# Batches 0 and 1 of q and k loaded as 2 KB runs and regrouped on chip; band mask by matmul, two AV buffers, idle matmuls ahead of the data, new filler counts, two output tiles

## The chip, the cores and the metric

The kernel runs on one core of a Trainium2 chip. The metric is device time in microseconds (us) of one launch. Each version was executed several times; the kernel before takes 373.0 to 375.9 us. The profile is one of those executions, and its span is about 2 us shorter than the time. Engines: PE is TensorE (matmul), PEld its weight loads, DVE VectorE, ACT ScalarE, POOL GpSimd, SP the queue that stores the output.

## The reference, cut to what matters

```
q, k, v: [8 batches, 8 heads, 576 tokens, 64] f32
out_d    = softmax attention over means of 4 tokens (144 per head), repeated 4 times
out_local= softmax attention over tokens with |i - j| < 4 (a band)
x   = (out_d + out_local) as [4608, 512]
out = gelu(x @ w_in) @ w_out          # w_in 512x2048, w_out 2048x512
```

The kernel works in 9 chunks of 512 tokens. `m1(c)` is the first matmul of chunk c with its Gelu, `m2(c)` the second, 64 matmuls of 128x512 each, 0.216 us apiece at full clock. While chunk c is in m1, batch c+1 is brought in (transposed, summed in fours); while it is in m2, batch c+1 goes through attention. Batch 0 has nothing to hide behind: it is the prologue.

## The kernel before

The parts that matter: batch 0's loads are 256-byte runs, the band mask is built by six selections on GpSimd (POOL) and multiplied in by VectorE, and large matmuls ("fillers") are placed between the steps of the attention so that TensorE doesn't wait.

```python
def load_qk0(p):                                   # batch 0: 16 DMAs of 256-byte runs
    for nm, src in (("qn", q), ("kn", k)):
        for h in (2 * p, 2 * p + 1):
            nc.gpsimd.dma_start(out=ld[0][nm][:, :, h, :],
                                in_=src[0, h].rearrange("(c s) d -> s c d", s=CH))
# ... cut ...
def t_in(b, p, which):                             # batches 1 to 7: tokens to columns
    tr = ppool.tile([128, 1024], F16, tag="tr")    # one buffer
    for c in range(NCK):                           # 6 transposes of 96 tokens
        nc.tensor.transpose(tr[:, CH*c:CH*c+CH], nat[:, c, 2*p:2*p+2, :], I128[0:CH, 0:CH])
    # ... q: copy to qT, sums of four; k: two copies to kz, sums of four to kdz (cut)
# ... cut ...
def attn(b, fill, n0, n1, n2):
    fill(n0); scores(b, 0); fill(n1); mask(0); s_lo(b)
    for p in range(NP):
        if p + 1 < NP:
            scores(b, p + 1)
            if p + 2 == NP: to_gelu()              # ScalarE's table, 1.28 us
        else:
            fill(2)
        av(b, p)
        if p + 1 < NP: mask(p + 1)
        fill(n2)                                   # 7
        t_out(b, p)                                # transposes nall, the result of av
# ... cut ...
osb = wpool.tile([128, 512], F32, tag="osb", bufs=3)   # output tiles
```

The softmax here doesn't subtract the row's maximum and nothing guards it: scores larger than these inputs give would overflow.

## Time and profile before

| stage, from the timeline | us |
|---|---|
| prologue (batch 0), up to the first m1 matmul | 39.8 |
| chunk 0, input part of batch 1 beside m1 | 22.0 |
| chunk 0, attention of batch 1 beside m2 | 26.0 |
| six steady periods (batches 2 to 7) | 225.7 (37.6 each) |
| last two chunks and the end | 59.2 |
| span | 372.7 |

The windows view gives the two parts of chunk 0. Columns: window, length, busy time of PE, PEld, DVE, ACT and POOL with instruction counts, granted TensorE clock (1.00 is full), mean busy DMA share, GB/s.

```profile
39.80:61.80 22.00, 19.47 (x114) 8.58 (x113) 13.49 (x24) 9.23 (x16) 13.54 (x18) 0.88 1.76 162
61.80:87.80 26.00, 22.60 (x224) 13.08 (x223) 14.37 (x22) 13.09 (x26) 16.01 (x18) 1.00 1.18 110
```

TensorE's clock can be read from the length of equal matmuls. These lines are of the timeline of the kernel before (start, length, engine, line, operation, tiles, shapes, count, and in brackets the idle time and what ended it):

```profile
12.62 0.49 PE L298 MATMUL sc<-qT,kz 128*128 128x116 f16 x3
...
24.50 0.59 PE L252 MATMUL vd_ps<-v_win,Gb 128*128 128x512 f16 x1 [0.23 <-DMA v_win<-in_v_dram]
...
39.76 8.44 PE L170 MATMUL m_ps<-xT,w_in_sb 128*128 128x512 f16 x26
```

The same three score matmuls take 0.32 us in a group later on. So the prologue ran at half clock up to about 28 us, although the windows view writes 1.00 for it; m1 also began at half clock: 26 matmuls in 8.44 us, where full clock needs 5.6. The second line shows what batch 0 waited for: v_win, which landed at 24.5 us.

In the steady periods TensorE had one clear wait. The chain of waits of one period (start, length, what) leaves TensorE after the last scores, goes through ScalarE and VectorE, and comes back with the last output transpose:

```profile
148.29 0.19 PE tr_o L351
...
152.43 0.23 PE sc L304 x4
...
153.04 0.73 ACT e L312
...
154.25 1.00 ACT L365
...
155.75 0.47 ACT out_sb L193
156.22 0.19 ACT xd L357
...
156.43 0.76 DVE xT L358
157.19 0.16 DVE rr L342
...
157.38 1.10 DVE nall L344
...
158.53 0.23 PE tr_o L351
```

From the end of the last scores (152.66) to the last transpose (158.53) are 5.9 us, and the filler work placed there is about 1 us too short.

### The profile page before, as it was taken

How to read it: one execution, taken by the hardware profiler on the slowest of the kernel's cores; microseconds unless marked ns; L12 is line 12 of the kernel's file. 1: busy time of each engine (PE TensorE's matmuls, PEld its weight loads, DVE VectorE, ACT ScalarE, POOL GpSimd, SP SyncE). 2: the span in 40 equal slices, each digit the busy share in tenths (PEclk: the TensorE clock that was granted, in tenths of full speed). 3: DMA queues.
4: the chain of work that ended last, by engine and by line, in shares of the span. 5: the costliest groups of instructions: out<-in, count | busy, mean ns of one | idle time of the engine just before them, and what ended most of it. 6: DMA issues, size and time to landing. Idle time of an engine off the chain costs nothing.

```text
span 372.7 us, 6854 instructions
## 1 busy us (share of the span) xinstructions
PE 337.7 (91%) x2812; PEld 187.1 (50%) x2812; DVE 186.1 (50%) x318; ACT 193.3 (52%) x366; POOL 187.8 (50%) x254
## 2 busy tenths in 40 slices
PE   1764888879999999999999999999999999999995
PEld 1634344545565556555554556455645564444442
DVE  5327278483757276728672857285728572000000
ACT  2634244554575457545763676357635763623721
POOL 8993937761396639662976298529762100000000
PEclk9998599999999999999999999999999999999999
DMA  7999999991099809980999099909990002002002
GB/s 50 83 147 190 138 194 134 140 95 58 0 97 155 124 2 93 162 123 2 88 163 126 2 80 165 131 1 78 166 132 2 4 30 84 0 30 84 0 30 84
DMA packets 134383, 32.30 MB, mean 87 GB/s; under 512 B 118608, under 2 KB 129872, under 8 KB 134352
## 3 DMA queue, kind: packets, MB, share of 16 engines
q0 software_dynamic: 129024, 22.43, 78.3%
q1 hardware_dynamic: 5184, 9.31, 7.0%
q8 instruction: 22, 0.36, 0.4%
q10 hardware_dynamic: 144, 0.13, 0.1%
q14 instruction: 9, 0.07, 0.1%
HBM read 44.83 MB, written 9.44 MB: 146 GB/s over the span
## 4 chain that ended last, share of the span: by engine, by line
PE 75%; DVE 9%; ACT 7%; POOL 5%; issue 2%; DMA 1%; ACTq 0%; DVEq 0%; POOLq 0%
PE m_ps L170 32%; PE m_ps L182 27%; DVE nall L344 3%; PE sc L298 3%; ACT L365 2%; DVE xT L358 2%; PE sc L304 2%; PE tr_o L354 2%; PE tr_k L202 2%; PE tr_q L202 2%; ACT e L312 2%; POOL k_nat L106 2%; POOL q_nat L106 2%; PE tr_o L351 1%; DMA v_win<-in_v_dram 1%
## 5 line engine op out<-in xcount | busy, mean ns | idle before, releaser
L170 PE MATMUL m_ps<-xT,w_in_sb 128*128 128x512 f16 x576 | 137.7, 384 | 0.0
L182 PE MATMUL m_ps<-w_out_sb,gT 128*128 128x512 f16 x576 | 133.9, 379 | 0.0
L173 ACT ACTIVATE gT<-m_ps 128x512 f16<-128x512 f32 x144 | 86.0, 597 | 59.3 <-PE m_ps L170 59.3
L182 PEld LDWEIGHTS <-gT 128*128 128x128 f16 x576 | 53.5, 98 | 57.3 <-issue 1.0
L170 PEld LDWEIGHTS <-w_in_sb 128*128 128x128 f16 x576 | 53.7, 99 | 56.8 <-issue 3.6
L212 POOL TENSOR_TENSOR q_t<-qT 128x288 f32<-128x288 f16 x24 | 16.0, 665 | 66.2 <-DVE qT L205 51.9
L193 ACT COPY out_sb<-m_ps 128x512 f32<-128x512 f32 x35 | 20.5, 586 | 44.6 <-PE m_ps L182 44.6
L221 DVE TENSOR_REDUCE kdz<-kz 64x144 f16<-64x576 f16 x56 | 41.8, 747 | 1.8
L83 POOL DMA_DIRECT2D q_nat<-in_q_dram x42 | 32.6, 790 | 10.1 <-PE m_ps L170 4.2
L344 DVE TENSOR_TENSOR nall<-av,rr 128x896 f16<-128x896 f32 x32 | 34.9, 1091 | 1.1
L358 DVE TENSOR_TENSOR xT<-tr_o,xd 128x576 f16<-128x576 f16 x32 | 24.2, 758 | 21.5 <-ACT xd L357 21.5
L217 DVE COPY kz<-tr_k 64x576 f16<-64x576 f16 x56 | 25.4, 454 | 18.4 <-PE tr_k L202 17.5
L83 POOL DMA_DIRECT2D k_nat<-in_k_dram x42 | 32.2, 783 | 4.6 <-DMA w_in_sb<-in_moe_w_in_dram 3.6
L320 DVE TENSOR_TENSOR e<-e,band 128x1152 f16<-128x1152 f16 x32 | 24.7, 773 | 16.6 <-ACT e L313 16.0
L205 DVE COPY qT<-tr_q 128x576 f16<-128x576 f16 x28 | 12.8, 458 | 36.4 <-PE tr_q L202 35.7
L188 DVE COPY out_sb<-m_ps 128x256 f32<-128x256 f32 x1 | 0.4, 425 | 58.4 <-PE m_ps L182 58.4
L357 ACT COPY xd<-tr_o 128x144 f16<-128x144 f16 x32 | 8.9, 279 | 38.1 <-PE tr_o L354 38.1
L95 POOL DMA_DIRECT2D v_win<-in_v_dram x30 | 26.7, 927 | 1.3 <-DMA k_nat<-in_k_dram 1.3
L312 ACT ACTIVATE e<-sc 128x680 f16<-128x680 f32 x32 | 23.4, 732 | 0.0
L351 PE MATMUL tr_o<-I,nall 128*128 128x128 f16 x32 | 7.5, 233 | 14.5 <-DVE nall L344 13.9
L272 POOL TENSOR_TENSOR v_t<-v_grp 128x1024 f32<-128x1024 f16 x6 | 12.7, 2115 | 14.5 <-DMA v_grp<-in_v_dram 14.5
L313 ACT ACTIVATE e<-sc 128x472 f16<-128x472 f32 x32 | 18.2, 570 | 0.0
(91 smaller groups left out, 397.8 us busy)
## 6 DMA issues: line engine op xcount, KB each, us to landing
out_dram<-out_sb SPq DMA_DIRECT2D x35, 256.0 KB, 3.4
v_win<-in_v_dram POOLq DMA_DIRECT2D x40, 128.0 KB, 9.5
q_nat<-in_q_dram POOLq DMA_DIRECT2D x42, 96.0 KB, 4.0
k_nat<-in_k_dram POOLq DMA_DIRECT2D x42, 96.0 KB, 4.6
v_grp<-in_v_dram POOLq DMA_DIRECT2D x6, 512.0 KB, 8.4
w_in_sb<-in_moe_w_in_dram POOLq DMA_DIRECT2D x4, 512.0 KB, 9.9
w_out_sb<-in_moe_w_out_dram POOLq DMA_DIRECT2D x4, 512.0 KB, 10.5
q_nat<-in_q_dram POOLq DMA_DIRECT2D x8, 72.0 KB, 3.1
```

The costliest lines, as they stand in the source:

```text
L83: nc.gpsimd.dma_start(out=ld[b % 2][nm][:, c, :, :], in_=src[b, :, CH * c:CH * c + CH, :].rearrange("h s d -> s h d"))
L95: nc.gpsimd.dma_start(out=L["vw"][:, j, :, 0:64], in_=v[b, :, W0[j]:W0[j] + 128, :].rearrange("h s d -> s h d"))
L170: nc.tensor.matmul(out=ps, lhsT=w_in_sb[:, fc, 128 * j:128 * j + 128], rhs=xT[:, fc, 512 * c:512 * c + 512], start=(fc == 0), stop=(fc == 3))
L173: nc.scalar.activation(out=g[:, j, :], in_=ps, func=ACTF.Gelu)
L182: nc.tensor.matmul(out=ps, lhsT=g[:, j, 128 * t:128 * t + 128], rhs=w_out_sb[:, j, :], start=(j == 0), stop=(j == NJ - 1))
L193: nc.scalar.copy(out=osb, in_=ps)
L217: nc.vector.tensor_copy(out=kz[r, p, hh, :], in_=tr[r, 0:S])
L221: nc.vector.tensor_reduce(out=kdz[r, p, hh, :], in_=kz[r, p, hh, :].rearrange("p (g r) -> p g r", r=4), axis=AX.X, op=ALU.add)
L312: nc.scalar.activation(out=e2[:, :, 0:340], in_=sc2[:, :, 0:340], func=ACTF.Exp, scale=0.125)
L320: nc.vector.tensor_tensor(out=e2, in0=e2, in1=band.unsqueeze(1).broadcast_to([128, 2, S]), op=ALU.mult)
L344: nc.vector.tensor_tensor(out=nall.rearrange("p j a c -> p a j c"), in0=av4[:, :, :, 0:64], in1=rr.unsqueeze(3).broadcast_to([128, 2, 7, 6 ...
L358: nc.vector.tensor_tensor(out=xT[:, p, S * b:S * b + S].rearrange("p (g r) -> p g r", r=4), in0=tr[:, 0:S].rearrange("p (g r) -> p g r", r=4),
```

## The change

Its intent: load q and k of batches 0 and 1 in runs of 8 tokens (2 KB instead of 256 B), so that GpSimd issues 8 DMAs instead of 16 for batch 0 and v_win comes earlier; put the tokens in order on chip by a VectorE regroup copy and eight transposes of 72; take the sums of four by accumulating matmuls; add the band mask inside the score accumulation; let TensorE run idle matmuls until data comes; and re-tune the fillers. To make room in the on-chip memory, two output tiles are used instead of three. Cut to its core:

```diff
-            "qn": ipool.tile([CH, NCK, H, 64], F16, tag="qn", name="q_nat"),
+            "qn": ipool.tile([CH, 4096], F16, tag="qn", name="q_nat"),
+    def load_qk8(b, p):
+        for nm, src in (("kn", k), ("qn", q)):
+            nc.gpsimd.dma_start(
+                out=nat8(ld[b][nm])[:, 2 * p:2 * p + 2, :, :].rearrange("p h r d -> p h (r d)"),
+                in_=src[b, 2 * p:2 * p + 2].rearrange("h (p r) d -> p h (r d)", r=8))
# ... cut: band selections replaced by two on a 128x128 tile B0; v_win issued ahead of Gb ...
+    def t_in8(b, p, which):
+        rr8 = wpool.tile([72, 8, 2, 64], F16, tag="nr", bufs=2, name="nat_r")
+        nc.vector.tensor_copy(out=rr8, in_=nat[:, 2*p:2*p+2, :, :].rearrange("p h r d -> p r h d"))
+        # PSUM: b == 0: one of two "mm" buffers; b == 1: the single "tr" buffer
+        tok = tr[:, 0:S].rearrange("p (r t) -> p t r", r=8)
+        for r in range(8):
+            nc.tensor.transpose(tr[:, 72 * r:72 * r + 72], rr8[:, r, :, :], I128[0:72, 0:72])
+        for g in range(2):
+            for r in range(4):
+                nc.tensor.matmul(out=trf[:, 288 + g:432:2], lhsT=rr8[:, 4 * g + r, :, :],
+                                 rhs=I128[0:72, 0:72], start=(r == 0), stop=(r == 3))
+        # q: copies to qT (from tok, a step of 72) and qd; k: to kz (from tok) and kdz
# ... cut ...
-        ps = ppool.tile([128, 512], F32, tag="mm", bufs=2, name="vd_ps")
+        va = ppool.tile([128, 1024], F32, tag="av", name="va")     # v sums: both halves
# ... cut ...
+            if b == 0:                                     # in scores: the band mask
+                nc.tensor.matmul(out=dst, lhsT=I128, rhs=nb[:, x:x + QW[j]], start=True, stop=False)
# ... cut: odd AV pairs of batch 0 in the two "mm" buffers ...
-                fill(2)
+                fill(4)
-            fill(n2)
+            fill(n2 if p + 1 < NP else n2 + 4)
# and in chunk 0, for batch 1:
-                f2(12)
+                f2(8)
-                attn(b, f2, 4, 9, 4)
+                attn(b, f2, 2, 9, 7)
# ... cut ...
-    osb = wpool.tile([128, 512], F32, tag="osb", bufs=3, name="out_sb")
+    osb = wpool.tile([128, 512], F32, tag="osb", bufs=2, name="out_sb")
+    spin(10)                                               # ten idle matmuls at the start
-                attn(b, f2, 6, 9, 7)
+                attn(b, f2, 6, 9, 8)
```

For batch 1 the order in m1 becomes 16 large matmuls, then eight times one `t_in8` and five large matmuls.

## The prediction

> **What bounds the kernel now.** From the chain of waits, three stages. (1) Prologue: the first large matmul (m1 of chunk 0) starts at 39.8 us. (2) Chunk 0 with batch 1 beside it, 39.8 to 87.8 us: 48.0 us. (3) Six steady periods of 37.6 us to 313.6, then two plain chunks of 27.6 us and a tail. In (3) TensorE sets the time: in the timeline its starts follow each other without a gap except before the last output transpose, which waits about 1.0 us per period for `nall` (the waits view says 0.8 because it counts modelled ends).
>
> **Steady periods: the sure gain.** 4 fill matmuls instead of 2 before the last AV, 12 instead of 7 after it, 8 instead of 7 elsewhere, at 0.216 us each. The chain that holds the last transpose (end of the last scores, three exponentials, table load, out_sb, xd, xT, reciprocal, nall) is 5.9 us; the work placed over it becomes about 6.5 us. The wait goes: 36.7 us a period, -5.5 us over six.
>
> **Prologue: less than it looks.** Removed: 256-byte loads (16 issues of 0.73 us become 8 of about 0.65), six band selections on POOL (2.2 us), four mask multiplies (0.75 us each) on VectorE. v_win landed last at 24.5 us and held batch 0; I estimate it at 16-17 us, no longer the limit. Added on VectorE: regroup copies, and strided reads of PSUM. The Trainium skill (VectorE: DVE Perf Modes, "What auto-detection actually checks") gives 16-bit operands double rate only at step +-1. The kz copy from PSUM takes 0.454 us contiguous; with a step of 72 it should fall to the 0.75 us that the one-per-cycle 576-element operations take here. The regroup copy, contiguous inside, should take about 0.42 us. So each pair costs VectorE's chain about 0.42 + 0.76 (TensorE) + 1.5 + 0.42 us plus waits behind scores, which carry ten more matmuls (+0.5 us): pairs done at about 21 us, first AV near 26 us (26.5 before). After it, no masks and two AV buffers save about 2 us; the Gelu table load still stands before the first xd. m1 starts near 37.5 us: -2.
>
> **Chunk 0 with batch 1: about even, or worse.** Its input part becomes one chain per pair through the single `tr` buffer: regroup, TensorE 0.72, kz 1.5, kdz 0.55, regroup, TensorE 0.72, qT 0.75, qd 0.28: about 5.4 us against 3.68 now; TensorE has 3.2 us of work for it. Input part +4 to +6 us. The attention part gains 3 to 4 us (its five waits of 0.7 to 1.1 us are filled). Now twelve m1 matmuls run at 427 ns up to 45 us, with the granted clock at 0.74 over 30-50 us. I expect this again: TensorE stays mostly idle just before m1, so the idle matmuls warm only the start (Trainium skill, TensorE: Matmul & The Clock Gate, Part 1: the gate closes again after an idle window). Net +1.5 us.
>
> **Tail:** separate output tiles let both last copies run together, -0.4 us.
>
> **Sum:** -5.5 - 2 + 1.5 - 0.4 = about -6.5 us: 368.5 us, range 362.5 to 373.5. Faster by over 2%: 0.40; within: 0.56; slower: 0.04.
>
> **What would show it.** Right: period 36.7 and no wait before the last tr_o; kz 0.75 us; regroup 0.4 us; v_win no releaser of TensorE; first m1 at 36-39 us at 427 ns; batch 1's pairs 5 us apart. Wrong: kz at 0.45 us (then 2.4 us less in the prologue and up to 4 in batch 1), or a full clock at m1's start.
>
> **What would make it wrong.** Strided PSUM reads at double rate; regroup slower; 2 KB loads landing late; the clock falling in batch 1's gapped input part, which would add several us.

## The result, and the profile after

The changed kernel took 387.5 us (384.91 to 390.71, 4 runs); in the same rounds the kernel before took 374.89 (374.48 to 375.38). The ratio is 1.0313 with a 95% interval of 1.0256 to 1.0369: 3% slower, outside the predicted range. A ratio here is the mean time of one kernel's fast runs over that of the other's of the same rounds, so not quite the ratio of the medians quoted. One of the four runs counts as slow by the rule (1.5% above the fastest) and is left out of the ratio. The profiled run is the fastest of the four.

| stage, us | before | after | difference | predicted |
|---|---|---|---|---|
| prologue | 39.8 | 48.9 | +9.1 | -2 |
| chunk 0, input part | 22.0 | 31.0 | +9.0 | +4 to +6 |
| chunk 0, attention part | 26.0 | 22.9 | -3.1 | -3 to -4 |
| six steady periods | 225.7 | 220.9 | -4.8 | -5.5 |
| last two chunks and the end | 59.2 | 59.2 | 0.0 | -0.4 |
| span | 372.7 | 382.9 | +10.2 | |

The windows of chunk 0's two parts in the changed kernel: the attention part is now TensorE nearly throughout, and in the input part TensorE is busy for only 23 of 31 us.

```profile
48.90:79.90 31.00, 23.14 (x195) 12.22 (x193) 17.20 (x38) 9.23 (x16) 16.81 (x20) 0.93 1.11 77
79.90:102.80 22.90, 22.22 (x224) 13.12 (x223) 11.87 (x18) 13.09 (x26) 0.00 (x0) 1.00 0.09 36
```

**Prologue.** One pair of heads of batch 0 in the timeline of the changed kernel, from its kz copies to those of the next pair:

```profile
12.00 1.52 DVE L261 COPY kz<-m_ps 64x576 f16<-64x576 f16 x2 [2.46 <-PE m_ps L253]
...
13.56 0.42 DVE L240 COPY nat_r<-q_nat 72x1024 f16<-72x1024 f16 x1
...
14.04 0.66 PE L250 MATMUL m_ps<-I,nat_r 72*128 72x72 f16 x8 [2.07 <-DVE nat_r L240]
...
14.50 1.16 PE L253 MATMUL m_ps<-I,nat_r 72*128 72x72 f16 x8
...
17.61 0.69 PE L250 MATMUL m_ps<-I,nat_r 72*128 72x72 f16 x8
18.10 1.02 PE L253 MATMUL m_ps<-I,nat_r 72*128 72x72 f16 x8
19.16 1.52 DVE L261 COPY kz<-m_ps 64x576 f16<-64x576 f16 x2 [4.85 <-PE m_ps L253]
```

The q step of TensorE starts at 14.04, the scores run from 15.40 to 17.61 (2.2 us), the next k step from 17.61 to 19.1. VectorE sits idle for 4.85 us of the 7.2 until TensorE is done. The copies cost what was predicted (kz 0.76 us each, regroup 0.42); TensorE's steps cost twice what was predicted, and it is at half clock here. When the clock fell is in the windows view of the changed kernel:

```profile
6.00:7.00 1.00, 0.83 (x16) 0.64 (x15) 0.13 (x1) 0.00 (x0) 1.00 (x3) 1.00 0.94 112
7.00:8.00 1.00, 0.00 (x0) 0.00 (x0) 0.99 (x2) 0.00 (x0) 1.00 (x2) 1.00 0.93 138
8.00:8.50 0.50, 0.00 (x0) 0.00 (x0) 0.47 (x2) 0.01 (x1) 0.50 (x2) 1.00 1.04 148
8.50:9.00 0.50, 0.10 (x2) 0.10 (x3) 0.50 (x2) 0.49 (x2) 0.50 (x1) 0.62 0.77 117
```

The ten idle matmuls had raised the clock by 6 us. TensorE then did one step, waited 2.1 us for VectorE, and was at half clock when it went on. Half clock isn't the whole of the prologue: from 8.62 us to m1 the mean granted clock is 0.67 in the windows view, so about two thirds of that time is at half clock.

The end of the pairs is not the last delay. TensorE forms the v sums only then, in the two halves of one PSUM tile, and waits for ScalarE and VectorE ahead of the first AV; the kernel before has no wait of TensorE between its v sums and its first AV.

```profile
34.60 0.38 PE L276 MATMUL va<-v_win,GL 128*128 128x512 f16 x1 [0.92 <-ACT v_d L274]
35.84 0.19 PE L358 MATMUL av<-v_d,ed 128*128 128x65 f16 x1 [0.85 <-DVE v_lm L278]
```

**Chunk 0, input part.** One pair of batch 1 in the timeline of the changed kernel, from kz to the next kz: 6.2 us.

```profile
55.36 1.52 DVE L261 COPY kz<-t_k 64x576 f16<-64x576 f16 x2 [4.39 <-PE t_k L253]
...
57.55 0.42 DVE L240 COPY nat_r<-q_nat 72x1024 f16<-72x1024 f16 x1
...
58.03 0.43 PE L250 MATMUL t_q<-I,nat_r 72*128 72x72 f16 x8 [1.63 <-DVE nat_r L240]
...
58.30 0.67 PE L253 MATMUL t_q<-I,nat_r 72*128 72x72 f16 x8
...
59.00 0.76 DVE L256 COPY qT<-t_q 128x576 f16<-128x576 f16 x1 [1.03 <-PE t_q L253]
...
59.89 0.63 DVE L240 COPY nat_r<-k_nat 72x1024 f16<-72x1024 f16 x1
...
61.55 1.52 DVE L261 COPY kz<-t_k 64x576 f16<-64x576 f16 x2 [1.03 <-PE t_k L253]
```

Each VectorE step waits for TensorE (1.03 us) and each TensorE step for VectorE (1.63 us): one after the other, through one PSUM buffer. The eight sum matmuls (L253) last 0.67 us as a group, the eight transposes of the same 72 columns (L250) 0.43.

**Steady periods.** The wait of the last transpose is gone, and a new one has come. Chain of waits of the changed kernel, third period, and then the one line that the waits view has for TensorE over all six periods (engine, line, waited for: us in total, times, longest), first of the kernel before, then of the changed kernel:

```profile
170.85 5.72 DMA out_dram<-out_sb
176.67 0.59 ACT out_sb L209
177.31 0.59 PE m_ps L184 x2
```

```profile
PE tr_o L351 <- DVE nall L344: 5.0, 6, 0.8
PE m_ps L184 <- ACT out_sb L209: 2.8, 5, 0.8
```

With two output tiles, the ScalarE copy of the last tile waits for an output DMA, and the next m1 waits for that copy.

### The profile page after: what moved, and what is told of

It reads as the page before. It is cut to its first block, busy times and chain, and to the rows that moved or that the text cites. A ratio compares the mean times of both kernels' runs of the same rounds, so it can differ in the third digit from the quotient of the medians.

```text
span 382.9 us, 7183 instructions
## 1 busy us (share of the span) xinstructions
PE 349.8 (91%) x2974; PEld 202.1 (53%) x2974; DVE 190.6 (50%) x339; ACT 192.9 (50%) x366; POOL 176.4 (46%) x238
## 4 chain that ended last, share of the span: by engine, by line
PE 79%; DVE 7%; ACT 5%; DMA 5%; issue 3%; ACTq 0%; DVEq 0%
PE m_ps L184 31%; PE m_ps L196 27%; PE sc L319 5%; DMA out_dram<-out_sb 5%; DVE kz L261 2%; PE av L366 2%; PE m_ps L253 2%; PE tr_q L218 2%; PE tr_k L218 2%; PE tr_o L389 2%; DVE nat_r L240 1%; ACT L400 1%; PE sc L324 1%; ACT out_sb L209 1%; PE m_ps L250 1%
## 5 line engine op out<-in xcount | busy, mean ns | idle before, releaser
L233 DVE TENSOR_REDUCE kdz<-kz 64x144 f16<-64x576 f16 x48 | 35.9, 747 | 1.5
L379 DVE TENSOR_TENSOR nall<-av,rr 128x896 f16<-128x896 f32 x30 | 32.7, 1091 | 1.0
L96 POOL DMA_DIRECT2D q_nat<-in_q_dram x36 | 27.9, 788 | 6.5 <-DMA w_out_sb<-in_moe_w_out_dram 3.6
L229 DVE COPY kz<-tr_k 64x576 f16<-64x576 f16 x48 | 21.9, 455 | 18.2 <-PE tr_k L218 17.5
L319 PE MATMUL sc<-qT,kz 128*128 128x112 f16 (+1 forms) x320 | 28.8, 223 | 0.0
L344 DVE TENSOR_TENSOR e<-e,band 128x1152 f16<-128x1152 f16 x28 | 21.0, 751 | 15.5 <-ACT e L337 15.5
L96 POOL DMA_DIRECT2D k_nat<-in_k_dram x36 | 27.7, 788 | 1.5 <-DMA v_win<-in_v_dram 1.5
L319 PEld LDWEIGHTS <-kz 128*128 128x128 f16 x320 | 23.3, 103 | 0.8
L336 ACT ACTIVATE e<-sc 128x680 f16<-128x680 f32 x32 | 23.4, 731 | 0.0
L335 ACT ACTIVATE ed<-sc 128x288 f16<-128x288 f32 x32 | 13.0, 408 | 19.5 <-PE sc L319 19.5
L221 DVE COPY qT<-tr_q 128x576 f16<-128x576 f16 x24 | 11.0, 458 | 19.1 <-PE tr_q L218 18.5
```

Source lines behind the costliest of these rows:

```text
L96: nc.gpsimd.dma_start(out=nat6(ld[b % 2][nm])[:, c, :, :], in_=src[b, :, CH * c:CH * c + CH, :].rearrange("h s d -> s h d"))
L229: nc.vector.tensor_copy(out=kz[r, p, hh, :], in_=tr[r, 0:S])
L233: nc.vector.tensor_reduce(out=kdz[r, p, hh, :], in_=kz[r, p, hh, :].rearrange("p (g r) -> p g r", r=4), axis=AX.X, op=ALU.add)
L319: nc.tensor.matmul(out=dst, lhsT=kz[:, p, hh, W0[j]:W0[j] + 128], rhs=qT[:, p, Q0[j]:Q0[j] + QW[j]], start=(b > 0), stop=True)
L336: nc.scalar.activation(out=e2[:, :, 0:340], in_=sc2[:, :, 0:340], func=ACTF.Exp, scale=0.125)
L379: nc.vector.tensor_tensor(out=nall.rearrange("p j a c -> p a j c"), in0=av4[:, :, :, 0:64], in1=rr.unsqueeze(3).broadcast_to([128, 2, 7, 6 ...
```

## The experiments

All twelve gave correct results. Each was run four times (a profile and three rounds). "Ratio" is against the kernel before of the same rounds. The stages in the table are those of each profiled run; the times move by 1% between runs of the versions whose clock falls, so a difference of less than 2 us in a stage is not read where the clock differs. The prologue of the kernel before, unaltered in a1_fills, measured 39.8 and 40.9.

| run | median us | ratio, interval | prologue | input part | attention part | six periods |
|---|---|---|---|---|---|---|
| a1_fills | 365.46 | 0.977, 0.973 to 0.981 | 40.9 | 21.9 | 24.8 | 217.3 |
| a2_osb3 | 383.74 | 1.017, 1.011 to 1.023 | 47.7 | 32.4 | 22.9 | 217.3 |
| a3_b1_old | 377.61 | 1.007, 1.001 to 1.013 | 46.5 | 20.8 | 22.9 | 222.6 |
| a4_b0_old | 380.94 | 1.017, 1.013 to 1.021 | 42.2 | 31.9 | 22.9 | 222.6 |
| b1_maskmul | 387.84 | 1.034, 1.031 to 1.038 | 47.6 | 35.5 | 22.9 | 221.6 |
| b2_warm | 379.66 | 1.015, 1.011 to 1.019 | 41.0 | 31.6 | 22.9 | 221.6 |
| b3_contig | 381.77 | 1.017, 1.011 to 1.023 | 45.7 | 32.0 | 22.9 | 221.2 |
| b6_tailspin | 362.66 | 0.968, 0.966 to 0.970 | 39.4 | 20.1 | 24.8 | 217.3 |
| c1_two_tr | 378.60 | 1.012, 1.009 to 1.015 | 47.3 | 23.4 | 22.9 | 221.5 |
| c3_nospin | 388.14 | 1.036, 1.033 to 1.040 | 49.9 | 32.7 | 22.9 | 221.0 |
| c2_new_all | 361.55 | 0.965, 0.962 to 0.968 | 40.3 | 20.1 | 23.1 | 217.3 |
| c4_old_all | 361.06 | 0.965, 0.962 to 0.967 | 37.6 | 20.1 | 24.8 | 217.3 |

Theories after the result. For the prologue: TensorE at half clock makes its steps the chain; rival: VectorE's copies are the chain whatever the clock. For chunk 0: the chain through one PSUM buffer; rival: the clock or the load itself. For the periods: the fillers are worth more than was seen, and the lost output tile takes part of it back.

### a1_fills: the new fillers alone, on the kernel before

```diff
-                fill(2)
+                fill(4)
-            fill(n2)
+            fill(n2 if p + 1 < NP else n2 + 4)
-                attn(b, f2, 6, 9, 7)
+                attn(b, f2, 6, 9, 8)
```

> The kernel before with only the new filler counts of the steady periods (4 ahead of the last AV, 12 after it, 8 elsewhere; three output buffers as before). If the steady part of the prediction holds: the period falls from 37.6 to 36.4-36.8 us, the wait of the last output transpose is gone, and the whole is 4.8 to 6.5 us faster than before (about 369 us). If fillers only move the wait elsewhere: within 2 us of before.

The ratio is 0.977, about 8.7 us of 374.75: more than expected. The period is 36.2 us instead of 37.6. The fillers are a clear gain by themselves (whether it is over 2% the interval leaves open). They gain more than expected because every output transpose waited a little, not only the last: in the chain before, the first tr_o matmul of the other pairs takes 0.19 us where it takes 0.06 here. Three times 0.13 us is most of the 0.5 us a period that the estimate lacked. The waits view, with its modelled matmul ends, shows no wait of TensorE at all in a1's periods. The attention part of batch 1 gained 1.2 us too.

### a2_osb3: three output tiles in the changed kernel

```diff
-                        osb = wpool.tile([128, 512], F32, tag="osb", bufs=2, name="out_sb")
+                        osb = wpool.tile([128, 512], F32, tag="osb", bufs=3, name="out_sb")
# ... the last block's two half tiles come from the same pool, for space ...
```

> The changed kernel with three output buffers again instead of two. The changed kernel shows TensorE waiting in all 2.8 us at the start of m1 for the ScalarE copy of an output tile that waits for an output DMA. If the lost buffer is the cause: steady periods of 36.3-36.5 us instead of 36.8 on average, all in all 2 to 3 us faster than the changed kernel. If the DMA is only late and the wait would be there anyway: no change.

The periods fall from 36.8 to 36.2 us, exactly those of a1, and no wait of TensorE is left in them. So the third output tile is worth 3.6 us (220.9 to 217.3), more than the 2 to 3 expected. The other runs with two tiles have 221.0 to 222.6. Two of its four runs count as slow by the rule; their mean clock was 0.94 against 0.96 in the other two, so the whole time says less than the stage.

### a3_b1_old: batch 1 brought in as before

```diff
-    for p in range(NP):
-        load_qk8(1, p)
+    run(load_qk(1))
# ... and in m1 of chunk 0 the old t_in with the old filler counts in place of t_in8 ...
```

> The changed kernel with batch 1 loaded and brought in as before (256-byte runs, six transposes per tensor, sums by VectorE reduce). Theory: the one-buffer chain of the regrouped input part (about 6 us per pair) costs chunk 0 its 5.6 us, so this run is 4 to 8 us faster than the changed kernel (379-383 us), with pairs of batch 1 3.7 us apart again. Rival: the chunk is slower because of the clock or the filler counts, then this run is within 2 us of the changed kernel.

The input part is 20.8 us instead of 31.0, and the ratio falls from 1.031 to 1.007, about 9 us. The new input part of batch 1 costs about 10 us, more than the 8 expected at most. Nothing was lost by the old 256-byte loads: in the waits view of this stage TensorE waits for VectorE alone (2.2 us, at tr_k).

### a4_b0_old: batch 0 as before, the rest changed

```diff
-    load_qk8(0, 0)
+    load_qk0(0)
# ... all of the old prologue: loads, t_in0, VectorE mask, one AV buffer, no idle matmuls;
# ... kept: v sums through the "av" tile, batch 1, fillers, two output tiles ...
```

> The changed kernel with batch 0 as in the kernel before (loads, six transposes, VectorE mask, one AV buffer, no idle matmuls), the rest as changed. Theory: the prologue alone costs 9.3 us, so first m1 near 39.8 us and the whole 8 to 11 us faster than the changed kernel, about 376 us, near the kernel before. Rival: half of the loss would come back, because a late prologue overlaps with loads that would be late anyway; then 380 us or more.

380.94 us: a gain of about 5 us, less than the theory's 8 to 11. By its number the rival (380 us or more) came out; but the prologue itself is 42.2 us, between the two. The run is not quite the old prologue: the v sums still go through both halves of one PSUM tile, and TensorE waits there 0.7 us for the ScalarE copy of the first half (it did not before). The last v_win tile also lands later, at 25.2 us against 24.5. VectorE's first reciprocal comes at 29.27 us, at 27.73 in the kernel before. Two output tiles cost 1.7 us more here than in the changed kernel. So about 7 us of the prologue's 9 go with the new prologue; of the 2.4 us left, up to 1.5 go with these two delays, and the rest is open.

### b1_maskmul: the mask by VectorE again

```diff
-            if b == 0:
-                nc.tensor.matmul(out=dst, lhsT=I128, rhs=nb[:, x:x + QW[j]], start=True, stop=False)
+    mask(0)      # four multiplies of 0.76 us, between the steps of the prologue
```

> The changed kernel with the band mask of batch 0 again as a VectorE multiply (four of 0.76 us) in place of ten mask matmuls per pair. Theory (TensorE at half clock is on the prologue's chain): each set of scores falls from 2.2 us to about 1.3 us, first m1 1 to 3 us earlier than the 46.5-48.9 us of the changed kernel. Rival (VectorE's copies are the chain): the four multiplies add 3 us to it, first m1 2 to 3 us later.

The scores did fall, from 2.2 to 1.25 us, but the prologue is 47.6 us, within the 46.5 to 48.9 us that the unaltered prologue shows in four runs (the changed kernel, a2, a3, c1). Neither the theory's 1 to 3 us earlier nor the rival's 2 to 3 us later came out. The mask matmuls neither cost nor save time that could be seen; that VectorE spends what TensorE saves would fit, and is not shown. The longer input part (35.5 us) came with a mean clock of 0.75 there.

### b2_warm: idle matmuls where TensorE waits

```diff
     for w in "kq":
+        if w == "q":
+            spin(8)
         t_in8(0, p, w)
```

> The changed kernel with eight more idle matmuls ahead of each q input step of batch 0, where TensorE waits 2.1 us for VectorE. Theory (half clock makes the chain long): the clock stays full from 6 us on, input steps fall from 1.6 to 0.8 us and scores from 2.2 to 1.1, first m1 at 40-43 us instead of 46.5-48.9, 5 us off the whole. Rival (the chain is VectorE's whatever the clock): first m1 within 1.5 us of the changed kernel, or later where the idle matmuls are in the way.

The prologue is 41.0 us, 5.5 to 8 us shorter, as the clock theory says and against the rival. In the timeline of b2_warm an input step takes 0.73 us from its start to that of the next step (8.91 to 9.64), about half of the changed kernel's 1.37 (8.90 to 10.27):

```profile
8.91 0.43 PE L250 MATMUL m_ps<-I,nat_r 72*128 72x72 f16 x8 [0.35 <-DVE nat_r L240]
9.17 0.67 PE L253 MATMUL m_ps<-I,nat_r 72*128 72x72 f16 x8
9.64 0.46 PE L250 MATMUL m_ps<-I,nat_r 72*128 72x72 f16 x8
```

Once raised by the first ten idle matmuls, the clock stays full up to 38.1 us; it is half from there into m1. Yet even so the new prologue is no shorter than the old one (39.8).

### b3_contig: the sums written side by side

```diff
-                nc.tensor.matmul(out=trf[:, 288 + g:432:2], lhsT=rr8[:, 4 * g + r, :, :],
+                nc.tensor.matmul(out=trf[:, 288 + 72 * g:360 + 72 * g], lhsT=rr8[:, 4 * g + r, :, :],
# ... and the copies to qd and kdz interleave the two groups ...
```

> The changed kernel with the group sums written side by side in PSUM (72 columns of one group of tokens, then the other) and interleaved by the copies that read them[...]. In the changed kernel a sum matmul, written with a step of two, starts every 0.066 us at full and 0.12 us at half clock, twice the transposes of the same 72 columns (0.030 and 0.060). If the step of the write halves the rate: both equal, 0.26 us less per tensor at full and 0.48 us at half clock; chunk 0's input part 2 us shorter, first m1 2 to 3 us earlier, 4 to 5 us in all. If the fp32 accumulation itself costs it: no change.

The rate doubled. In b3_contig's timeline the eight sum matmuls start 0.26 us before what follows them (55.45 to 55.71), as long as the eight transposes take (55.18 to 55.45); in the changed kernel, at the same clock, they took 0.46 to 0.47.

```profile
55.18 0.43 PE L250 MATMUL t_q<-I,nat_r 72*128 72x72 f16 x8 [1.63 <-DVE nat_r L240]
55.45 0.42 PE L253 MATMUL t_q<-I,nat_r 72*128 72x72 f16 x8
55.71 1.25 PE L184 MATMUL m_ps<-xT,w_in_sb 128*128 128x512 f16 x5
```

So a step of two in the fp32 output halves the rate, and the accumulation does not. The ratio fell from 1.031 to 1.017, about 5.4 us and so a little more than the 4 to 5 expected, but the parts do not all show it: the input part did not shrink (mean clock 0.81 there against 0.93). While the clock was full, a pair took 5.5 us (kdz at 54.04 and 59.56) instead of 6.2. The local cost is shown, its share of the whole is not settled, because the clock moves with it.

### b6_tailspin: idle matmuls ahead of batch 0's output transposes, on a1

```diff
     av(0, 2)
+    spin(6)
     t_out(0, 2)
     av(0, 3)
+    spin(6)
     t_out(0, 3)
# ... likewise ahead of t_out(0, 0) and t_out(0, 1) ...
```

> The kernel before with the new filler counts (run a1) and, as the one thing more, 5 or 6 idle matmuls ahead of each of batch 0's four output transposes, where TensorE waits 1.4 to 2 us for VectorE. If the clock falls there because TensorE is idle: it stays full from 28 us on and the first m1 matmuls run at 0.216 us instead of 0.427, 2 to 3 us less than run a1 (363 us). If the clock does not follow from this idleness: half clock at m1's start again, and no gain.

The windows view of a1_fills, then of b6_tailspin, same stretches:

```profile
36.00:40.00 4.00, 1.86 (x25) 1.71 (x25) 2.69 (x4) 0.28 (x1) 3.02 (x4) 0.50 2.21 145
40.00:44.00 4.00, 3.77 (x15) 1.75 (x16) 0.93 (x2) 0.88 (x2) 4.00 (x7) 0.50 1.76 122
```

```profile
36.00:40.00 4.00, 3.39 (x41) 2.11 (x42) 2.11 (x4) 0.56 (x2) 3.28 (x5) 1.00 2.22 144
40.00:44.00 4.00, 3.49 (x17) 1.52 (x16) 0.65 (x1) 2.08 (x4) 4.00 (x6) 1.00 1.72 138
```

The clock stays full (0.50 became 1.00), and the 23 m1 matmuls from 40.70 us on take 5.12 us, 0.22 apiece. The whole is 362.66 us, ratio 0.968 against a1's 0.977, about 3.4 us. The four runs also lie within 0.4 us, where a1's spread over 2.4.

### c1_two_tr: a second PSUM buffer and the regroup one tensor ahead, batch 1 only

```diff
+            if which == "q":
+                trf = ppool.tile([128, 1024], F32, tag="av", name="t8_q")[:, 0:512]
+            else:
+                trf = ppool.tile([128, 512], F32, tag="tr", name="t8_k")
+        nxt = regroup(*ahead) if ahead else None      # before this tensor's copies out
```

> The changed kernel; batch 1's input part alone is given a second PSUM buffer (q in the then idle AV buffer, k in tr) and issues the regroup copy one tensor ahead, so that TensorE's step no longer stands between two VectorE steps. In the changed kernel a pair takes 6.1-6.2 us, VectorE is busy for about 4.0 us of it (two regroups 0.85, kz 1.5, kdz 0.6, qT and qd 1.05) and TensorE for about 3.8. Theory (the chain through one buffer): pairs 4 to 4.6 us apart, chunk 0's input part 23-26 us instead of 31-32, 5 to 8 us off the whole. Rival (VectorE's or TensorE's load itself, or the clock): pairs stay above 5.5 us and the whole within 2 us.

Pairs are now 4.4, 4.0 and 4.9 us apart (kz at 53.19, 57.63, 61.60 and 66.52 us in c1_two_tr's timeline):

```profile
53.19 1.52 DVE L270 COPY kz<-t_k 64x576 f16<-64x576 f16 x2 [3.21 <-PE t_k L261]
...
57.63 1.51 DVE L270 COPY kz<-t_k 64x576 f16<-64x576 f16 x2
...
61.60 1.52 DVE L270 COPY kz<-t_k 64x576 f16<-64x576 f16 x2
...
62.79 2.12 POOL L302 TENSOR_TENSOR v_t<-v_grp 128x1024 f32<-128x1024 f16 x1 [1.81 <-DMA v_grp<-in_v_dram]
...
63.79 1.39 DVE L240 COPY nat_r<-k_nat 72x1024 f16<-72x1024 f16 x1
...
66.52 1.51 DVE L270 COPY kz<-t_k 64x576 f16<-64x576 f16 x2
```

The input part is 23.4 us instead of 31.0, and the whole about 7 us faster than the changed kernel. The chain of TensorE and VectorE taking turns was the cause. The edit frees it in two ways at once, by the second buffer and by the earlier regroup, and what each is worth was not tried. With the chain gone, VectorE and TensorE are both near their load. The last pair shows another limit: a regroup copy of 0.42 us took 1.39 us beside a GpSimd addition (62.79 to 64.91), and ended 0.27 us after it. In c3_nospin a copy beside another such addition took 1.50 us and also ended 0.27 us after it; beside GpSimd's DMA issues the copies of c1_two_tr took 0.54 to 0.81 us. The Trainium skill (GPSIMD Engine Reference, "Specifications") says that GpSimd shares its SBUF interfaces with VectorE, in contention with VectorE instructions in a 2-port mode; the slow copies fit that, and no run here isolates it.

### c3_nospin: without the ten idle matmuls

```diff
-    spin(10)
```

> The changed kernel without its ten idle matmuls. In the changed kernel they warm the clock for the first input step only (full from about 6 us, half again from 8.9). Theory: their worth is one tensor's step, 0.8 us, within the 1.5 us by which first m1 varies: first m1 at 47-50 us and the whole the same within 1%. Rival (they are what keeps the prologue from being worse): first m1 beyond 51 us.

388.14 us, ratio 1.036 against 1.031: the two intervals overlap. As placed, the idle matmuls were worth nothing that can be told from the spread.

### c2_new_all and c4_old_all: the best of each prologue

c2_new_all is the new prologue with b2's idle matmuls, more ahead of the output transposes, b3's sums, a3's batch 1 and a2's output tiles:

```diff
+        if w == "q":
+            spin(8)
+    spin(6, "sc")      # ahead of t_out(0, 1) to t_out(0, 3), 8 at the first
# ... and the edits of a2_osb3, a3_b1_old and b3_contig ...
```

> The changed prologue kept busy (eight idle matmuls ahead of each q step as in run b2, more ahead of the output transposes), sums side by side, batch 1 brought in as before, three output buffers. Theory: first m1 at 39-41 us and at full clock, chunk 0 at 45 us, periods of 36.2 us: 361 to 365 us, so with its side costs removed the new prologue is worth no more than the old one (run b6: 362.7). Rival (2 KB loads are worth something once the clock is full): 359 us or less.

c4_old_all is b6 with v_win issued ahead of the band selections and idle matmuls at the start:

```diff
+    load_vw(0)
     for pat, base, cm in ((-1, 3, 1), (1, 3, -1)):     # the band selections
-    load_vw(0)
+    spin(10)
     t_in0(0, 0)
+    spin(8)
     t_in0(0, 1)
# ... mask(0) and mask(1) moved behind the last t_in0 ...
```

> Run b6 (kernel before, new filler counts, idle matmuls ahead of the output transposes) with v_win issued ahead of the six band selections, the first two masks moved behind the last input step, and 10 and 8 idle matmuls ahead of the first two input steps. v_win landed last at 24.5 us and held batch 0; it should land about 1.9 us earlier and the first AV start at 24-25 us: first m1 at 37-38 us, 1.5 to 2.5 us faster than b6, about 360.5-361 us. If something else holds it next (POOL's selections for the mask, VectorE): within 1 us of b6.

361.55 and 361.06 us, ratios 0.9646 and 0.9645: both beat both kernels, and they cannot be told apart. They are not equal by stage: c4's prologue is 2.7 us shorter, and c2's attention part 1.7 us. c2 keeps the changed kernel's filler counts for batch 1 (8; 2, 9, 7) and c4 the old ones (12; 4, 9, 4), so the comparison favours the new prologue, if anything; c4 with the new counts was not run. The theory's number for c2 came out (361 to 365 expected), the rival's (359 or less) did not: with its side costs removed, the new way of bringing in batch 0 is worth no more than the old one. In c4 the prologue fell to 37.6 us, as expected; its time missed the expected 361 by a hair.

## Why the prediction was wrong

Of the 16.7 us between the sum predicted (-6.5) and the span measured (+10.2), 11.1 lie in the prologue and 4.4 in chunk 0. Point by point, against "Sum: -5.5 - 2 + 1.5 - 0.4":

1. **The step that failed first: "Prologue: less than it looks ... m1 starts near 37.5 us: -2."** It measured +9.1 us, and all of it arises ahead of the first AV: that came at 35.84 us, against "first AV near 26 us" (26.50 in the kernel before); from there to m1 are 13.1 us, 13.3 before (11.5 predicted, 11.4 in b2_warm). The cost of VectorE's copies was right (kz 0.76 us, regroup 0.42 us, v_win no longer waited for). What failed is "0.76 (TensorE)" and the +0.5 us for the mask matmuls: they are full-clock sizes, and most of the prologue is at half clock. An input step, from its start to the copy of its result, measured 1.6 us (0.97 at full clock, from 5.90 to 6.87 us), and a set of scores 2.2 us. The trace before showed it: its score matmuls took 0.49 us early and 0.32 us later. The prediction said that "the idle matmuls warm only the start" but then used warm sizes for the rest. b2_warm confirms the cause: with the clock full up to 38.1 us the prologue is 41.0 us. Even that is 3.5 us above the prediction, so the chain itself was also drawn too short: pairs were 3.8, 5.4 and 5.1 us apart in b2_warm against the 3.1 us and some waits that the estimate assumed. b2's own idle matmuls are not in that: after each group of eight TensorE still waits 0.34 to 0.82 us for VectorE. The last kz ended at 22.7 us there, 1.7 later than "about 21 us"; about 2 us more were lost up to the first AV at 29.69, where TensorE waits 0.96 and 0.85 us at the v sums. The prediction has no term for that wait.
2. **"Chunk 0 with batch 1: about even, or worse ... Net +1.5 us."** It measured +5.9. The mechanism was right, and c1_two_tr shows it: one chain through the single buffer. The mis-sized term is "about 5.4 us" per pair: it measured 6.2, mostly because a TensorE step with strided sums is 1.03 us from regroup to copy, not 0.72 to 0.76 (b3_contig shows the halved rate of strided fp32 writes), so 3 us over four pairs. The attention part gained 3.1 us, as said. 1.2 of it come with the filler counts that a1_fills has too; the rest came with batch 1's own counts and the other edits, which no run tried apart.
3. **"Steady periods: the sure gain ... -5.5 us."** The fillers alone are worth 8.4 us (225.7 to 217.3, a1_fills); three small waits of 0.13 us a period, which the waits view hides, were left out. The changed kernel keeps only 4.8 of it, because the prediction overlooked a term: the diff takes away one of three output tiles, and a2_osb3 shows 3.6 us for it. That the total was near (-4.8) is luck: the two errors cancel.
4. **"Tail: separate output tiles let both last copies run together, -0.4 us."** Nothing was gained (59.2 us both times). The ScalarE copy still starts only when the VectorE copy has ended (379.14 + 0.42, then 379.60), as before. Both read one PSUM tile; that this is the reason was not tested.
5. The prediction named "the clock falling in batch 1's gapped input part" as a risk. It did fall in some runs (mean 0.75 in b1_maskmul, 0.93 in the profiled run of the changed kernel). This kernel's times spread over 6 us, and its slowest run has the lowest mean clock (0.934) and its fastest the highest (0.960); that the clock makes the whole spread is not shown.

The Trainium skill helped in one place and was not enough in another. VectorE: DVE Perf Modes, "What auto-detection actually checks", gives a doubled rate to 16-bit data at a step of one, and its other doubled rate needs both sides in SBUF, so a strided read of PSUM has neither; the trace agrees (0.454 us at a step of one, 0.76 at 72). TensorE: Matmul & The Clock Gate, "HAM oscillation — how this bites in real kernels", warns of idle gaps over about 3.4 us; here the clock fell in a gap of 2.1 us.

## What to carry to other kernels

Before costing TensorE work, read from the lengths of equal matmuls which clock that stretch has, and put idle matmuls where TensorE waits, not only ahead of the first data. When a diff re-tunes several things, list what it takes away (here a third output tile and a second PSUM buffer) with the same care as what it adds. A load that is faster by itself buys nothing if putting the data in order becomes the new chain: here the fillers alone (a1_fills) were worth 2.3%, and idle matmuls in four places another 1%.

## What the Trainium skill lacked or had wrong

- TensorE: Matmul & The Clock Gate, "HAM oscillation — how this bites in real kernels", states the rule "no PE-idle gaps >~3.4µs". As a limit for one gap that is not enough: TensorE lost its full clock in gaps of 2.1 us (changed kernel, between 6.8 and 8.9 us) and 1.9 us (a1_fills, between 35.0 and 36.9 us). It gives no size for how busy TensorE has to be; the traces do. In them the clock holds for multiples of 3.41 us (in the changed kernel from 5.2 us on: 3.41, 10.24, 3.41, 10.24, 3.41, 3.41, 6.83, 6.83), and the busy share of TensorE in such a stretch, as this profile counts it, tells what follows. Of the 177 full-clock stretches among the first 18 of each of the 14 traces, all 25 with a busy share under 0.46 were followed by half clock, all 130 over 0.53 by full clock, and the 22 between went either way. The changed kernel's stretch from 5.21 to 8.62 us has 1.24 us busy of 3.41, a1_fills' from 32.33 to 35.74 has 1.21, and the same stretch of b6_tailspin, which kept its clock, 2.52.
- No page has the cost of a strided matmul output: with a step of two in fp32, a matmul of 72 columns starts every 0.062 us at full clock and 0.12 at half (changed kernel), about twice the 0.033 and 0.060 us of unit step (b3_contig).
- TensorE: Matmul & The Clock Gate has only a general caveat on clock events; no page says that a profile's granted clock can read 1.00 ahead of the first recorded change: in the kernel before it reads 1.00 up to 28 us, where a 128x512 matmul takes 0.59 us and later 0.38.
